# Gate and value of the last eight slices as seven block products, on input tiles of 768 tokens

## The chip, the cores and the metric

The kernel runs on one core of a Trainium2 chip. TensorE (PE) multiplies, VectorE (DVE), ScalarE (ACT) and GpSimd (POOL) work elementwise, SyncE (SP) issues the DMAs. The metric is the device time of one execution in microseconds; before the change its median over 3 runs is 1119.23 us (1118.88 to 1119.54).

## The reference

An attention with landmark means (Nystrom) over 8 batches, 8 heads, 576 tokens and 64 columns a head, whose output is the input of a gated MLP on 4608 tokens (model 512, hidden 1536):

```python
A = sm(q, k_lm); Bm = sm(q_lm, k_lm); C = sm(q_lm, k)      # 32 landmarks
for _ in range(6):
    Z = 2 * Z - Z @ Bm @ Z
attn = A @ Z @ C @ v                                       # -> x [4608, 512]
xn = x / sqrt(mean(x * x) + 1e-6) * rms_g
g = xn @ w_gate; val = xn @ w_val                          # 512 -> 1536 each
out = (g * sigmoid(g) * val) @ w_out                       # 1536 -> 512
```

The weights come as 64-bit floats and are decoded to 32 bits on the chip. Each 32-bit operand of the MLP is split into a high and a low float32r part, and a product is three matmuls: high x high, high x low, low x high.

## The kernel before

The hidden size is cut into 12 slices of 128. The kernel has two passes over the tokens, in chunks of 512 (nine in all).

**The early pass** does the attention and, chunk by chunk as the tokens become ready, the MLP of slices 0 to 3 (`early`). A partial sum [128 tokens x 512] is copied from PSUM by ACT (L294) and written to DRAM (`p_dram`, DMA pd<-ob). **The late pass** (L705 to L721) loads each chunk's inputs again (xf<-xd), splits them on ACT and DVE (L719, L720), computes slices 4 to 11, adds the partial sum on DVE (L297) and writes the output.

`mlp_chunk` (L250) makes, for each slice, 12 matmuls for gate (psg) and 12 for value (psv): four blocks of 128 of the model dimension, three matmuls each, 512 tokens wide. Then ACT takes the Silu of the gate (L268), DVE multiplies by the value (L269), and the hidden value is split (L273, L274). When all slices of the chunk are done, 12 matmuls a slice make the four output groups of 128 tokens (pso). All matmuls go through one line, L137, and PE executes them in the order in which they are written. A matmul has a weight load (PEld) ahead of it.

**What sets the order.** `Mixer` (L211) weaves the attention and the weight decoding into the MLP. It has a clock that moves by MMT = 0.216 for each matmul of `fill` (L238), and streams that say with `yield` how long they want to wait before their next piece. NW (L491) is such a wait: in `newton` (L463) it stands between the transposes, sums and maxima on DVE (BT, den) and the first product p0 (L492, the trace calls it p). WAIT1 and WAIT2 space the weight decoding of the late pass. ACT and DVE also work in one fixed order each, which a list scheduler makes at build time; PE's order is kept as written.

`Weights.load_next` (L176) decodes one 128 x 512 weight block: Abs on ACT (L187), four DVE operations (L188 to L195), then the split into high and low (L201, L202).

## Time and profile before

| | |
|---|---|
| median of 3 runs | 1119.23 us |
| profiled execution, its own time | 1122.06 us |
| its span, first to last instruction | 1120.3 us |
| first matmul of the late pass | at 528.0 us |
| PE, DVE, ACT busy over the span | 93%, 51%, 27% |
| DVE busy from 528 us on | 188.9 of 592 us |
| granted PE clock, mean; from 528 us on | 0.959; 1.00 |

A row of the timeline is: start, length, engine, line, operation, output <- inputs, sizes, count. Matmuls are pipelined, so a matmul's length (0.39 us for 512 columns) is longer than the step from one to the next; the step is read from the starts. A row of the groups ends with the busy time, the mean in ns, and the idle time of the engine ahead of it with what ended it. A window's row has the busy time and count of each engine, the granted clock and the DMA share.

### The profile page before, as it was taken

How to read it: one execution, taken by the hardware profiler on the slowest of the kernel's cores; microseconds unless marked ns; L12 is line 12 of the kernel's file. 1: busy time of each engine (PE TensorE's matmuls, PEld its weight loads, DVE VectorE, ACT ScalarE, POOL GpSimd, SP SyncE). 2: the span in 40 equal slices, each digit the busy share in tenths (PEclk: the TensorE clock that was granted, in tenths of full speed). 3: DMA queues.
4: the chain of work that ended last, by engine and by line, in shares of the span. 5: the costliest groups of instructions: out<-in, count | busy, mean ns of one | idle time of the engine just before them, and what ended most of it. 6: DMA issues, size and time to landing. Idle time of an engine off the chain costs nothing.

```text
span 1120.3 us, 16081 instructions
## 1 busy us (share of the span) xinstructions
PE 1046.4 (93%) x6630; PEld 812.7 (73%) x6630; DVE 568.9 (51%) x1203; ACT 301.8 (27%) x614; POOL 87.6 (8%) x85
## 2 busy tenths in 40 slices
PE   5559888998998999999999999999999999999998
PEld 3336555675666677777788888888888888888887
DVE  7899978566666353799832423233232323323231
ACT  3446565445344433344110101111010111100010
POOL 2243121111021010100000000000000000000000
PEclk7669988998999899999999999999999999999999
DMA  9345533314211110664311030201102020010101
GB/s 328 124 161 167 174 133 123 123 59 139 96 60 43 39 61 20 249 194 147 130 57 57 3 111 1 82 31 57 57 6 107 1 85 29 20 57 1 38 1 38
DMA packets 44457, 95.41 MB, mean 85 GB/s; under 512 B 4832, under 2 KB 24288, under 8 KB 42208
## 3 DMA queue, kind: packets, MB, share of 16 engines
q1 hardware_dynamic: 44384, 94.39, 24.6%
q8 instruction: 52, 0.85, 0.3%
q14 instruction: 21, 0.17, 0.1%
HBM read 66.06 MB, written 28.31 MB: 84 GB/s over the span
## 4 chain that ended last, share of the span: by engine, by line
PE 73%; DVE 16%; DMA 5%; ACT 3%; issue 2%; POOL 1%; SPq 0%; ACTq 0%; DVEq 0%; POOLq 0%
PE psg L137 23%; PE pso L137 22%; PE psv L137 22%; DVE lmT L345 2%; PE pO L137 1%; DVE xr L590 1%; DVE w L192 1%; DMA qk<-in_q_dram 1%; PE pn L137 1%; DMA wrawg<-in_moe_w_gate_dram 1%; DMA wrawv<-in_moe_w_val_dram 1%; DVE w L195 1%; DVE h L274 1%; PE sC L137 1%; DVE mx L379 1%
## 5 line engine op out<-in xcount | busy, mean ns | idle before, releaser
L137 PE MATMUL pso<-whio,h 128*128 128x512 f32 x864 | 279.5, 399 | 3.5 <-ACT h L273 2.1
L269 DVE TENSOR_TENSOR s<-s,psv 128x512 f32<-128x512 f32 x108 | 74.0, 685 | 282.3 <-PE psv L137 267.1
L268 ACT ACTIVATE s<-psg 128x512 f32<-128x512 f32 x108 | 64.4, 597 | 502.4 <-PE psg L137 502.2
L137 PEld LDWEIGHTS pso<-whio,h 128*128 128x128 f32 x864 | 165.5, 192 | 41.9 <-ACT h L273 3.4
L137 PE MATMUL psg<-xhi,whig 128*128 128x512 f32 x432 | 173.3, 401 | 16.4 <-ACT xhi L616 16.4
L137 PE MATMUL psg<-xlo,whig 128*128 128x512 f32 x432 | 172.6, 400 | 2.6 <-DVE xlo L618 1.9
L137 PE MATMUL pso<-wloo,h 128*128 128x512 f32 x432 | 173.1, 401 | 0.0
L137 PE MATMUL psg<-xhi,wlog 128*128 128x512 f32 x432 | 172.5, 399 | 0.0
L137 PE MATMUL psv<-xhi,whiv 128*128 128x512 f32 x432 | 170.2, 394 | 0.0
L137 PE MATMUL psv<-xlo,whiv 128*128 128x512 f32 x432 | 169.9, 393 | 0.0
L137 PE MATMUL psv<-xhi,wlov 128*128 128x512 f32 x432 | 169.6, 393 | 0.0
L137 PEld LDWEIGHTS psg<-xhi,whig 128*128 128x128 f32 x432 | 82.1, 190 | 36.2 <-ACT xhi L616 16.9
L137 PEld LDWEIGHTS psg<-xlo,whig 128*128 128x128 f32 x432 | 82.1, 190 | 22.3 <-DVE xlo L618 2.7
L297 DVE TENSOR_TENSOR ob<-pt,pso 128x512 f32<-128x512 f32 x36 | 24.6, 687 | 144.6 <-PE pso L137 144.6
L137 PEld LDWEIGHTS psg<-xhi,wlog 128*128 128x128 f32 x432 | 82.1, 190 | 19.6 <-issue 2.5
L137 PEld LDWEIGHTS pso<-wloo,h 128*128 128x128 f32 x432 | 82.8, 192 | 17.7
L137 PEld LDWEIGHTS psv<-xhi,whiv 128*128 128x128 f32 x432 | 81.2, 188 | 18.6 <-issue 1.4
L137 PEld LDWEIGHTS psv<-xlo,whiv 128*128 128x128 f32 x432 | 81.3, 188 | 18.0 <-issue 0.8
L137 PEld LDWEIGHTS psv<-xhi,wlov 128*128 128x128 f32 x432 | 81.0, 188 | 18.0 <-issue 1.3
L274 DVE TENSOR_TENSOR h<-s,h 128x512 fp32r<-128x512 f32 x108 | 76.0, 704 | 10.7 <-ACT h L273 8.6
L618 POOL TENSOR_TENSOR xlo<-xr,xhi 128x512 fp32r<-128x512 f32 (+7 forms) x32 | 31.8, 1009 | 201.3 <-ACT xhi L616 201.1
L137 PE MATMUL pn<-PV 32*32 32x96 f32 (+1 forms) x768 | 27.1, 261 | 18.6 <-DVE PV L501 14.1
(135 smaller groups left out, 995.5 us busy)
## 6 DMA issues: line engine op xcount, KB each, us to landing
xd<-xr SPq DMA_DIRECT2D x8, 1152.0 KB, 4.5
pd<-ob SPq DMA_DIRECT2D x36, 256.0 KB, 2.6
pt<-pd SPq DMA_DIRECT2D x9, 1024.0 KB, 5.2
out_dram<-ob SPq DMA_DIRECT2D x36, 256.0 KB, 2.0
vt<-in_v_dram SPq DMA_DIRECT2D x16, 512.0 KB, 4.0
qk<-in_q_dram SPq DMA_DIRECT2D x14, 576.0 KB, 4.5
qk<-in_k_dram SPq DMA_DIRECT2D x14, 576.0 KB, 5.6
wrawg<-in_moe_w_gate_dram SPq DMA_DIRECT2D x12, 512.0 KB, 3.5
```

Of the source, the lines that this page charges most:

```text
L137: tc.keep_in_program_order(nc.tensor.matmul(*args, **kw))
L192: nc.vector.scalar_tensor_tensor(w, whead, 0x3FFFFFFF, w, op0=ALU.bitwise_or, op1=ALU.bitwise_and)
L195: nc.vector.scalar_tensor_tensor(w, wtail, 29, w, op0=ALU.logical_shift_right, op1=ALU.bitwise_or)
L268: nc.scalar.activation(s, banks[0], AF.Silu)
L269: nc.vector.tensor_mul(s, s, banks[1])
L274: nc.vector.tensor_sub(h2, s, h1.bitcast(F32))
L297: nc.vector.tensor_add(ob, part[:, t, :], ps)
L345: nc.vector.tensor_reduce(lmT[:, z], qk[z].rearrange("p h (m c) -> p h m c", c=LM), axis=AX.X, op=ALU.add)
L379: nc.vector.tensor_reduce(mx[:, e : e + 1], sC[e], axis=AX.X, op=ALU.max)
L590: last = nc.vector.scalar_tensor_tensor(xr[:, kk], xr[:, kk], gsb[:, kk : kk + 1], Rt, op0=ALU.mult, op1=ALU.mult)
L618: eng.tensor_sub(xlo[:, kk, off : off + n], xr[:, kk, pos : pos + n], xhi[:, kk, off : off + n].bitcast(F32),)
```

## The change

Slices 4 to 11 get another algorithm for gate and value. Write the weights of a slice as a 2 x 2 matrix of blocks (gate and value by the two halves of the model dimension, A11 A12 / A21 A22) and the inputs of 768 tokens as another (halves of the model dimension by two tiles of 384 tokens, B11 B12 / B21 B22). The four result blocks, gate and value of the two token tiles, then take seven block products instead of eight, in Winograd's form: P1 = A11 B11, P2 = A12 B21, and five products of combined blocks. A block product is 2 x 3 = 6 matmuls of 384 columns.

- `Fast.stream` decodes gate and value of a slice, combines them on DVE into S1 to S4 and splits seven blocks of 256 columns (high on ACT, low on DVE).
- `prepare` combines the inputs of a unit of 768 tokens in place and splits seven blocks of 768 columns (x1 to x7).
- `unit` writes the products of a slice into the banks px, pz and pw in the order 1, 5, 6, 2, 3, 7, with 4 of the slice before it after 5. Products 6, 7 and 4 are added to the bank of product 1, product 3 to that of 5. Between them ACT copies what a bank holds so far (c1, c2, c3) and DVE adds the next sum to the copy. The hidden values are then split, 384 columns at a time.
- The late pass becomes two passes of four slices each, over six units. The first adds to the early partial sums and writes a second set (`p2_dram`), the second adds to that and writes the output. Partial sums are loaded three groups ahead, 256 KB each.
- The first unit's inputs are prepared in the last early chunk, between its gate and value and its output products (`between`). The weights of the second pass's first slice and its output weights go to tiles of the early ones; three slices are decoded into tiles that come free in the sixth unit (`refill`).
- The pools: early inputs get a pool that is closed before `prepare`, attention pools move to the other end of SBUF, and a tile of 32 bytes is put in front of the late pool, so that its tiles start at multiples of 64 bytes. The attention tiles at that end start at 32 bytes past such a multiple.
- NW becomes 6.0, WAIT2 2.5.

The diff, cut to its core:

```diff
-NW = 2.0
+NW = 6.0
...
 WAIT1 = 4.0
-WAIT2 = 3.2
+WAIT2 = 2.5
...
+    mxs = ExitStack()
+    mx_ = mxs.enter_context(tc.tile_pool(name="mx", bufs=2, reuse_waits="tile"))
...
-    p_dram = [dram.tile([P, T // P, DM], F32, name=f"pd{i}", tag=f"pd{i}") for i in range(NCH)]
+    NG = NT // P
+    p_dram = [dram.tile([P, DM], F32, name=f"pd{i}", tag=f"pd{i}") for i in range(NG)]
+    p2_dram = [dram.tile([P, DM], F32, name=f"pe{i}", tag=f"pe{i}") for i in range(NG)]
...
+        between()
...
-                    if part is None:
-                        nc.scalar.copy(ob, ps)
-                        nc.sync.dma_start(p_dram[i][:, t, :], ob)
-                    else:
-                        nc.vector.tensor_add(ob, part[:, t, :], ps)
-                        r0 = T * i + t * P
...
+                    nc.scalar.copy(ob, ps)
+                    nc.sync.dma_start(p_dram[i * (T // P) + t], ob)
...
+    with tc.tile_pool(name="ap", bufs=1, side="right") as ap, tc.tile_pool(
+        name="sm", bufs=2, side="right"
     ) as sm, tc.tile_pool(name="pa", bufs=8 - GB, space=PSUM) as pa:
...
-            mix.fill(mlp_chunk(i, early, fs, *chunks.pop(i), None))
+            mix.fill(mlp_chunk(i, early, fs, *chunks.pop(i)))
             mix.drain(lambda: stage["second"] > i)
...
-    lp = ctx.enter_context(tc.tile_pool(name="lp", bufs=1))
-    late["p"] = lp
-    fl = list(range(NFA, NF))
-    later = Weights([(f, f if f < 2 * NFA else f - 2 * NFA) for f in fl])
-    later.plan([(f, nm) for f in fl[:NFA] for nm in "gvo"])
-    mix.add(later.stream(WAIT1))
-    for i in range(B - 1, NCH):
-        mix.fill(mlp_chunk(i, early, fs, *chunks.pop(i), None))
-    mix.drain(lambda: False)
-    later.plan([(f, nm) for f in fl[NFA:] for nm in "gv"] + [(f, "o") for f in fl[NFA:]])
-    mix.add(later.stream(WAIT2))
-    for i in range(NCH):
-        xf = lp.tile([P, NK, T], F32, name="xf", tag="xf", bufs=1)
+
+    al = ctx.enter_context(tc.tile_pool(name="al", bufs=1, side="right"))
+    nc.gpsimd.memset(al.tile([P, 8], F32, name="pad", tag="pad"), 0.0)
+    lp = ctx.enter_context(tc.tile_pool(name="lp", bufs=1, side="right", reuse_waits="tile"))
+    pl = ctx.enter_context(tc.tile_pool(name="pl", bufs=1, space=PSUM, reuse_waits="tile"))
+
+    TS = 384
+    NU = NT // (2 * TS)
+    SMMT = MMT * TS / T
...
+        def split(self, tile_, src):
+            nc.scalar.copy(tile_[:, 0], src)
+            nc.vector.tensor_sub(tile_[:, 1], src, tile_[:, 0].bitcast(F32))
...
+                self.fetch(f, "g")
+                self.fetch(f, "v")
+                yield -wait
+                g = self.decode(f, "g")
+                yield -wait
+                v = self.decode(f, "v")
+                yield -wait
+                ts = [place(c) for c in range(7)]
+                g0, g1, v0, v1 = g[:, : NK // 2], g[:, NK // 2 :], v[:, : NK // 2], v[:, NK // 2 :]
+                self.split(ts[A11], g0)
+                self.split(ts[A12], g1)
+                self.split(ts[A22], v1)
+                nc.vector.tensor_add(v1, v0, v1)
+                nc.vector.tensor_sub(v0, g0, v0)
+                yield -wait
+                nc.vector.tensor_sub(g0, v1, g0)
+                nc.vector.tensor_sub(g1, g1, g0)
+                self.split(ts[S1], v1)
+                self.split(ts[S3], v0)
+                self.split(ts[S2], g0)
+                self.split(ts[S4], g1)
+                self.done[f, "gv"] = ts
+                yield -wait
...
+        def get(self, f, what):
+            while (f, what) not in self.done:
...
+    gv_tags = [f"w{hl}{nm}{s}" for s in range(NFA) for hl in ("hi", "lo") for nm in "gv"]
+    o_tags = [(f"whio{s}", f"wloo{s}") for s in range(NFA)]
+    spare = gv_tags[7:]
+    lslot = [slot(lp, [f"fs{s}c{c}" for c in range(7)]) for s in range(NFA)]
+    fa, fb = list(range(NFA, 2 * NFA)), list(range(2 * NFA, 3 * NFA))
+    plan_a = [(f, "gv", lslot[s]) for s, f in enumerate(fa)]
+    plan_a += [(f, "o", oslot(lp, (f"lo{s}0", f"lo{s}1"))) for s, f in enumerate(fa)]
+    plan_b = [(fb[0], "gv", slot(wp, gv_tags[:7]))]
+    plan_b += [(f, "o", oslot(wp, o_tags[s])) for s, f in enumerate(fb)]
...
-        part = lp.tile([P, T // P, DM], F32, name="pt", tag="pt", bufs=2)
-        nc.sync.dma_start(part, p_dram[i])
-        xhi = mp.tile([P, NK, T], F32R, name="xhi", tag="xhi", bufs=XB)
-        xlo = mp.tile([P, NK, T], F32R, name="xlo", tag="xlo", bufs=XB)
-        for kk in range(NK):
-            nc.scalar.copy(xhi[:, kk], xf[:, kk])
-            nc.vector.tensor_sub(xlo[:, kk], xf[:, kk], xhi[:, kk].bitcast(F32))
-        mix.fill(mlp_chunk(i, later, fl, xhi, xlo, part))
+        return xf
...
+    def prepare(xf, xs):
+
+        h = NK // 2
+        b11, b12 = xf[:, :h, :TS], xf[:, :h, TS:]
+        b21, b22 = xf[:, h:, :TS], xf[:, h:, TS:]
+
+        def split(p, src):
+            t = lxs[0].tile([P, 2, h, TS], F32R, name=f"x{p}", tag=f"x{p}", bufs=1)
+            nc.scalar.copy(t[:, 0], src)
+            nc.vector.tensor_sub(t[:, 1], src, t[:, 0].bitcast(F32))
+            xs[p] = t
+
+        split(1, b11)
+        nc.vector.tensor_sub(b11, b12, b11)
+        split(5, b11)
+        yield
+        nc.vector.tensor_sub(b11, b22, b11)
+        split(6, b11)
+        yield
+        split(2, b21)
+        yield
+        split(3, b22)
+        nc.vector.tensor_sub(b12, b22, b12)
+        yield
+        split(7, b12)
+        yield
+        nc.vector.tensor_sub(b21, b21, b11)
+        split(4, b21)
...
+    of = {1: A11, 2: A12, 3: S4, 4: A22, 5: S1, 6: S2, 7: S3}
+
+    def product(ps, ws, xs, p, start):
+
+        w, x = ws[of[p]], xs[p]
+        h = NK // 2
+        for kk in range(h):
...
+                mm(
+                    ps,
+                    w[:, a, kk],
+                    x[:, b, kk],
+                    start=start and kk == a == b == 0,
+                    stop=kk == h - 1 and a == 1,
+                    skip_group_check=not start,
...
+    def unit(u, fs, xs, hs, src, last, after):
...
+        def close(fi, c1, px, ws):
+            yield from product(px, ws, xs, 4, False)
+            nc.vector.tensor_mul(c1, c1, px)
+            hs[fi, 0] = hidden(fi, 0, c1)
...
+        for fi, f in enumerate(fs):
+            ws = fast.get(f, "gv")
+            px = pl.tile([P, TS], F32, name="px", tag="px", bufs=2)
+            pz = pl.tile([P, TS], F32, name="pz", tag="pz", bufs=2)
...
+            yield from product(px, ws, xs, 1, True)
+            nc.scalar.copy(c1, px)
+            yield from product(pz, ws, xs, 5, True)
+            nc.scalar.copy(c3, pz)
+            if pend:
+                yield from close(*pend.pop())
+                after(fi - 1)
+            yield from product(px, ws, xs, 6, False)
+            nc.scalar.copy(c2, px)
+            pw = pl.tile([P, TS], F32, name="pw", tag="pw", bufs=1)
+            yield from product(pw, ws, xs, 2, True)
+            nc.vector.tensor_add(c1, c1, pw)
+            nc.scalar.activation(c1, c1, AF.Silu)
+            yield from product(pz, ws, xs, 3, False)
+            nc.vector.tensor_add(c2, c2, pz)
+            nc.scalar.activation(c2, c2, AF.Silu)
+            yield from product(px, ws, xs, 7, False)
+            nc.vector.tensor_add(c3, c3, px)
+            nc.vector.tensor_mul(c2, c2, c3)
+            hs[fi, 1] = hidden(fi, 1, c2)
+            pend.append((fi, c1, px, ws))
...
+        groups = list(range(half, ng)) + list(range(half))
+        nxt = prepare(load_next.pop(), xs_next) if load_next else iter(())
...
+        def part(t):
+            g = u * ng + t
+            ob = mp.tile([P, DM], F32, name="ob", tag=("ob", "s")[g % 2])
+            nc.sync.dma_start(ob, src[g])
...
+        def store(t):
+            g, ob = u * ng + t, obs[t]
+            nc.vector.tensor_add(ob, ob, bank.pop(t))
+            if not last:
+                nc.sync.dma_start(p2_dram[g], ob)
+                return
+            nc.sync.dma_start(out[g * P : (g + 1) * P, :], ob)
...
+        for t in groups[:3]:
+            part(t)
+        for fi in range(nf - 1):
+            yield from out_mm(groups[0], fi)
+        yield from close(*pend.pop())
+        after(nf - 1)
+        next(nxt, None)
+        for fi in range(nf - 1):
+            yield from out_mm(groups[1], fi)
+        next(nxt, None)
+        for n in (0, 1):
+            yield from out_mm(groups[n], nf - 1)
+            store(groups[n])
+            part(groups[n + 3])
+            next(nxt, None)
+        for n in range(2, ng):
+            for fi in range(nf):
+                yield from out_mm(groups[n], fi)
+            store(groups[n])
+            if n + 3 < ng:
+                part(groups[n + 3])
+            next(nxt, None)
+        for _ in nxt:
+            pass
+
...
+    xs_next, load_next, lxs = {}, [], []
+    mix.add(fast.stream(plan_a[:NFA], WAIT1))
+    for i in range(B - 1, NCH):
+        if i == NCH - 1:
+            first_x = load_x(0)
...
+        def between(i=i):
+            if i < NCH - 1:
+                return
+            mxs.close()
+            lxs.append(ctx.enter_context(tc.tile_pool(name="lx", bufs=1, reuse_waits="tile")))
+            for _ in prepare(first_x, xs_next):
+                pass
+            mix.add(fast.stream(plan_a[NFA:], WAIT1))
+
+        mix.fill(mlp_chunk(i, early, fs, *chunks.pop(i), between))
+    mix.add(fast.stream(plan_b, 2 * WAIT1))
+    freed = set()
+
+    def refill():
+        for s, f in enumerate(fb[1:]):
+            while s not in freed:
+                yield -0.3
+            yield from fast.stream([(f, "gv", lslot[s])], WAIT2)
+
+    mix.add(refill())
+    for n in range(2 * NU):
+        u, second_pass = n % NU, n >= NU
+        xs, hs = dict(xs_next), {}
+        xs_next = {}
+        if n + 1 < 2 * NU:
+            load_next.append(load_x((n + 1) % NU))
+        after = (lambda fi: freed.add(fi)) if n == NU - 1 else (lambda fi: None)
+        mix.fill(
+            unit(u, fb if second_pass else fa, xs, hs, p2_dram if second_pass else p_dram,
+                 second_pass, after),
+            SMMT,
+        )
```

How the order moves. On PE in the early pass, around p0 (the trace's p) of the seventh batch; sC and sA are scores of a later stage, pso is an output product of the fourth chunk. Before:

```order
L137 MATMUL pso<-wloo_1157,h_3354 128x512
L137 MATMUL pso<-whio_1156,h_3354 128x512
L137 MATMUL p_3545<-BT 32x32 x8
L137 MATMUL pso<-whio_1223,h_3429 128x512
L137 MATMUL pso<-wloo_1224,h_3429 128x512
L137 MATMUL pso<-whio_1223,h_3429 128x512
...
L137 MATMUL pso<-whio_1223,h_3429 128x512
L137 MATMUL sC<-qk_3417,lmT 32x288
L137 MATMUL sA<-qk_3417,lmT 32x288
...
L137 MATMUL sC<-lmT 32x32 x4
L137 MATMUL pso<-whio_1269,h_3525 128x512
L140 MATMUL sE<-ident,E 128x128 x4
```

Now:

```order
L141 MATMUL pso<-whio_1317,h_3591 128x512
L141 MATMUL sC<-qk_3482,lmT 32x288
L141 MATMUL sA<-qk_3482,lmT 32x288
...
L141 MATMUL sC<-lmT 32x32 x4
L141 MATMUL pso<-wloo_1318,h_3591 128x512
L144 MATMUL sE<-ident,E 128x128 x4
L144 MATMUL sF<-ident,E 64x128
L141 MATMUL pso<-whio_1317,h_3591 128x512
L141 MATMUL p_3696<-BT 32x32 x8
L141 MATMUL pso<-whio_1317,h_3591 128x512
```

p0 stood 15 MLP matmuls earlier, and ahead of the scores; now the scores and the first transposes (sE, sF) go first.

On PE in the late pass, one slice's gate and value; x1 to x7 are the split inputs, swfs0c0 the first combined weight block of the slot. Before, the gate's first three matmuls and the value's:

```order
L137 MATMUL psg_6794<-xhi_6752,whig5_5046 128x512
L137 MATMUL psg_6794<-xlo_6753,whig5_5046 128x512
L137 MATMUL psg_6794<-xhi_6752,wlog5_5047 128x512
...
L137 MATMUL psv_6807<-xhi_6752,whiv5_5085 128x512
L137 MATMUL psv_6807<-xlo_6753,whiv5_5085 128x512
L137 MATMUL psv_6807<-xhi_6752,wlov5_5086 128x512
```

Now, with the next slice's first two products:

```order
L141 MATMUL px_6479<-x1_6363,swfs0c0_5092 128x384 x6
L141 MATMUL pz_6480<-x5_6367,swfs0c4_5096 128x384 x6
L141 MATMUL px_6479<-x6_6381,swfs0c5_5097 128x384 x6
L141 MATMUL pw_6505<-x2_6391,swfs0c1_5093 128x384 x6
L141 MATMUL pz_6480<-x3_6401,swfs0c2_5094 128x384 x6
L141 MATMUL px_6479<-x7_6422,swfs0c6_5098 128x384 x6
L141 MATMUL px_6544<-x1_6363,swfs1c0_5263 128x384 x6
L141 MATMUL pz_6545<-x5_6367,swfs1c4_5267 128x384 x6
L141 MATMUL px_6479<-x4_6443,swfs0c3_5095 128x384 x6
L141 MATMUL px_6544<-x6_6381,swfs1c5_5268 128x384 x6
```

24 matmuls of 512 columns for 512 tokens have become 42 of 384 for 768 tokens, and a slice's fourth product stands after two of the next slice's.

On DVE in the sixth unit; sw are weights that are decoded for the second pass, c the copies of the accumulators, h hidden values:

```order
L727 TENSOR_SCALAR sw_7947<-sw_7947 128x512
L883 TENSOR_TENSOR c_7728<-c_7728,px 128x384
L730 SCALAR_TENSOR_TENSOR sw_7947<-srawg_7919,sw_7947 128x512
L726 TENSOR_SCALAR sw_7984<-sw_7984 128x512
L873 TENSOR_TENSOR h_7833<-c_7728,h_7833 128x384
L733 SCALAR_TENSOR_TENSOR sw_7947<-srawg_7919,sw_7947 128x512
L904 TENSOR_TENSOR c_7803<-c_7803,pw 128x384
L727 TENSOR_SCALAR sw_7984<-sw_7984 128x512
L907 TENSOR_TENSOR c_7804<-c_7804,pz 128x384
L730 SCALAR_TENSOR_TENSOR sw_7984<-srawv_7921,sw_7984 128x512
L910 TENSOR_TENSOR c_7805<-c_7805,px 128x384
L733 SCALAR_TENSOR_TENSOR sw_7984<-srawv_7921,sw_7984 128x512
```

The decoding's operations have come in between the additions to the accumulators' copies.

More of the change, by code (lines that the diff above doesn't have):

```diff
@@ L140, in tp @@
         tc.keep_in_program_order(nc.tensor.transpose(*args))
-    late = {}
     class Weights:
@@ L248, in nystrom_moe_kernel, with mlp_chunk @@
     mix = Mixer()
-    def mlp_chunk(i, wts, fs, xhi, xlo, part):
+    def mlp_chunk(i, wts, fs, xhi, xlo, between=lambda: None):
         nf = len(fs)
@@ L269, in mlp_chunk @@
                 nc.vector.tensor_mul(s, s, banks[1])
-                pool = mp if fi < NFA else late["p"]
-                h12 = pool.tile([P, 2, T], F32R, name=f"h{fi}", tag=f"h{fi}", bufs=1)
+                h12 = mp.tile([P, 2, T], F32R, name=f"h{fi}", tag=f"h{fi}", bufs=1)
                 h1, h2 = h12[:, 0], h12[:, 1]
-                (nc.scalar.copy if part is None else nc.vector.tensor_copy)(h1, s)
+                nc.scalar.copy(h1, s)
                 nc.vector.tensor_sub(h2, s, h1.bitcast(F32))
@@ new lines, in hidden, with out_mm @@
+    def hidden(fi, t, s):
+        if t == 0:
+            h12 = mp.tile([P, 2, T], F32R, name=f"h{fi}", tag=f"h{fi}", bufs=1)
+            hi, lo = h12[:, 0, :TS], h12[:, 1, :TS]
+        else:
+            hi, lo = (
+                wp.tile([P, T], F32R, name=f"h{fi}{n}", tag=spare[2 * fi + n], bufs=1)[:, :TS] for n in range(2)
+            )
+        nc.scalar.copy(hi, s)
+        nc.vector.tensor_sub(lo, s, hi.bitcast(F32))
+        return hi, lo
+    def unit(u, fs, xs, hs, src, last, after):
+        nf = len(fs)
+        pend = []
+        def close(fi, c1, px, ws):
[6 more added lines that the diff above has]
+            pz = pl.tile([P, TS], F32, name="pz", tag="pz", bufs=2)
+            c1, c2, c3 = (
+                lp.tile([P, TS], F32, name=f"c{n}", tag=f"c{n}", bufs=2 if n == 1 else 1) for n in (1, 2, 3)
+            )
+            yield from product(px, ws, xs, 1, True)
[19 more added lines that the diff above has]
+            pend.append((fi, c1, px, ws))
+        ng = 2 * TS // P
+        half = ng // 2
+        groups = list(range(half, ng)) + list(range(half))
+        nxt = prepare(load_next.pop(), xs_next) if load_next else iter(())
+        bank, obs = {}, {}
+        def part(t):
+            g = u * ng + t
+            ob = mp.tile([P, DM], F32, name="ob", tag=("ob", "s")[g % 2])
+            nc.sync.dma_start(ob, src[g])
+            obs[t] = ob
+        def out_mm(t, fi):
+            if t not in bank:
+                bank[t] = pg.tile([P, DM], F32, name="pso", tag="pg")
+            hi, lo = fast.get(fs[fi], "o")
+            h12 = hs[fi, t // half]
+            sl = slice(t % half * P, (t % half + 1) * P)
+            mm(bank[t], h12[0][:, sl], hi, start=(fi == 0), stop=False)
+            yield
+            mm(bank[t], h12[0][:, sl], lo, start=False, stop=False)
+            yield
+            mm(bank[t], h12[1][:, sl], hi, start=False, stop=(fi == nf - 1))
+            yield
+        def store(t):
[29 more added lines that the diff above has]
+            pass
```

89 lines of the change are left out of this document (72 added, 17 removed).

## The prediction

> **What bounds the kernel now.** First the page: span, engines, and the chain that ended last.
>
> ```profile
> span 1120.3 us, 16081 instructions
> PE 1046.4 (93%) x6630; PEld 812.7 (73%) x6630; DVE 568.9 (51%) x1203; ACT 301.8 (27%) x614; POOL 87.6 (8%) x85
> PE 73%; DVE 16%; DMA 5%; ACT 3%; issue 2%; POOL 1%; SPq 0%; ACTq 0%; DVEq 0%; POOLq 0%
> ```
>
> PE is busy for 93% of the span and holds 73% of the chain. A mean over both passes hides where PE is the limit, so next come the windows by stage (columns: PE, PEld, DVE, ACT, POOL busy with counts, granted clock, DMA share, GB/s).
>
> ```profile
> 139.00:215.00 76.00, 65.76 (x691) 43.10 (x692) 60.80 (x149) 39.43 (x84) 17.67 (x16) 0.87 0.38 130
> 215.00:269.00 54.00, 48.18 (x420) 35.30 (x418) 32.71 (x80) 24.14 (x55) 7.08 (x7) 0.94 0.30 98
> 269.00:326.00 57.00, 52.26 (x523) 36.97 (x522) 37.80 (x95) 25.54 (x58) 9.76 (x9) 0.97 0.26 92
> 528.00:1120.00 592.00, 588.52 (x2593) 486.07 (x2591) 188.90 (x318) 61.99 (x107) 0.00 (x0) 1.00 0.14 47
> ```
>
> The last row is the late pass. PE does not pause, the clock is full, DVE is at 32% and DMA at 14%. So there the number and the pace of matmuls set the time. The early rows are mixed: PE pauses and DVE works at 60 to 80%. The pace is read from the timeline of PE in the late pass, first and last of 15 rows:
>
> ```profile
> 799.73 0.39 PE L137 MATMUL psv<-xlo,whiv 128*128 128x512 f32 x1
> ...
> 802.90 0.39 PE L137 MATMUL psg<-xhi,whig 128*128 128x512 f32 x1
> ```
>
> Fourteen steps in 3.17 us are 0.2264 us; with 2592 matmuls (9 chunks of 8 slices of 36) in the 588 us that PE is busy, 0.2267. The 0.39 is a pipelined duration and no pace.
>
> **The change, part by part.** *Gate and value.* A slice on 768 tokens costs 36 matmuls of 512 columns before (24 x 1.5) and 7 x 6 = 42 of 384 after. There are 48 such slice-units (6 units, 8 slices). No row has 384 columns, so the pace lies between the 512 step and that of pO with 288 columns, here on PE and on the weight loads:
>
> ```profile
> 378.04 0.53 PE L137 MATMUL pO<-AS,Whi 64*128 64x288 f32 x4
> 378.41 0.29 PE L137 MATMUL pO<-AS,Wlo 64*128 64x288 f32 x2
> 378.28 0.19 PEld L137 LDWEIGHTS pO<-AS,Wlo 64*128 64x128 f32 x2
> ```
>
> The second pair of the first row ends at 378.57 and, at 0.29 each, began at 378.28; the next pair began at 378.41: 0.13 us for 288 columns (two half-height matmuls run side by side, so a pair is one step). From 288 to 512 columns, 0.13 to 0.2267, the line is 0.43 ns a column; at 384 it gives 0.172 to 0.173. I take 0.173. The bounds: 0.170 if the whole step shrinks with the columns (0.2267 x 0.75), 0.19 if the weight load, whose own rows last 0.19, became the pace. The third row speaks against that: the load began at 378.28 and its matmul at 378.41.
>
> Before: 48 x 36 x 0.2267 = 391.7 us. After: 48 x 42 x 0.173 = 348.8. The output products stay, 48 x 18 matmuls. **Gain 43**; bounds 49 (0.170) and 9 (0.19).
>
> The Trainium skill, "TensorE: Matmul & The Clock Gate", section "Back-to-back issue gap", gives N / 2.4 + 2.5 ns when warm: 215.8 ns at 512 columns, where this trace has 227, so the measurement decides. By the page, an estimate, 48 x (36 x 0.2158 - 42 x 0.1625) = 45 us would be gained.
>
> *What the products add on the other engines.* Each slice-unit now has on DVE three additions, two multiplications and two subtractions of 384 columns, on ACT three copies, two Silu and two casts. Each unit has seven splits of combined inputs (a cast on ACT, a subtraction on DVE) and four combinations on DVE, all of 768 columns, and six output additions. The nearest rows:
>
> ```profile
> L720 DVE TENSOR_TENSOR xlo<-xf,xhi 128x512 fp32r<-128x512 f32 x36 | 24.1, 685 | 0.0
> L422 DVE TENSOR_TENSOR AS<-AT,AS 128x576 fp32r<-128x576 f32 x16 | 12.0, 751 | 3.0 <-ACT AS L421 2.9
> L524 DVE TENSOR_TENSOR Wlo<-pW,Whi 128x256 fp32r<-128x256 f32 x8 | 3.3, 417 | 6.5 <-ACT Whi L523 6.5
> L268 ACT ACTIVATE s<-psg 128x512 f32<-128x512 f32 x108 | 64.4, 597 | 502.4 <-PE psg L137 502.2
> L556 ACT COPY xr<-pO 128x288 f32<-128x288 f32 x64 | 22.3, 405 | 21.4 <-PE pO L137 21.1
> ```
>
> From 256 to 512 and 576 columns DVE takes about 1.04 ns a column: 0.55 us for 384, 0.95 for 768. ACT at 384 lies between 0.405 and 0.597, about 0.49. A unit lasts 4 x (42 x 0.173 + 18 x 0.2267) = 45.4 us on PE; DVE needs 28 x 0.55 + 11 x 0.95 + 6 x 0.69 = 30.0 us, ACT under 20. This fits on average, so I cost it at nothing in the ten units without weight work. What hides it is PE's next products: a sum read from a bank has two to four products (1.04 us each) before that bank is written again. The tightest place is the first slice of a unit, where ACT's copy of product 1 has only product 5 to hide behind: 1.04 us against 0.49 and a semaphore on each side. If that cover went, 12 x 0.5 = 6 us.
>
> *Weights.* A slice now needs, beside two decodings, four combinations and seven splits of 256 columns:
>
> ```profile
> L188 DVE TENSOR_SCALAR w<-w 128x512 f32<-128x512 f32 x36 | 17.6, 488 | 8.8 <-ACT w L187 8.6
> L189 DVE TENSOR_SCALAR w<-w 128x512 int32<-128x512 int32 x36 | 16.9, 470 | 0.3
> L192 DVE SCALAR_TENSOR_TENSOR w<-wrawv,w 128x512 int32<-128x512 int32 x12 | 9.1, 758 | 0.2
> L195 DVE SCALAR_TENSOR_TENSOR w<-wrawg,w 128x512 int32<-128x512 int32 x12 | 8.2, 686 | 0.1
> ```
>
> That is 2 x 2.40 + 11 x 0.42 = 9.4 us of DVE a slice. Three slices are refilled in the sixth and seventh units, and in DVE's order their operations stand between the accumulator additions that PE waits for. Counted from the second slice of the sixth unit to the first of the seventh, DVE has 53 us of work in 45.4 us of PE. PE's lead of two products (2 us) takes some of the 7.6; the rest is late there. Around the first unit, where inputs and weights are prepared together, the backlog by the same count is at most 4 us. Bounds 0 and 11.6 us, with the handover above 17.6; I take **8 lost**, nearer the DVE count than nothing, since the order is fixed and DVE can't step aside.
>
> *DMA.* 28 MB more (inputs read twice, a second set of partial sums written and read) over some 550 us is 50 GB/s, beside 47 in the late row at a share of 0.14. It goes to 0.3 and stays covered. All of it is on SP's queue, where a store waits for its addition and holds up the loads behind it:
>
> ```profile
> pd<-ob SPq DMA_DIRECT2D x36, 256.0 KB, 2.6
> ```
>
> The partial sums are asked for three groups of 12 output matmuls (8 us) ahead, against 2.6 to land and 2.7 behind a store. I cost it at nothing; without that cover, 2.6 us a group.
>
> *The early pass.* NW moves p0 back. PE waits there, from 200 to 400 us:
>
> ```profile
> PE p L137 <- DVE BT L466: 13.2, 3, 5.8
> PE pn L137 <- DVE PV L501: 2.0, 1, 2.0
> ```
>
> p0 now stands 13, 15 and 21 matmuls later (the first pair of fences on the order shows the 15), which is 2.9 to 4.8 us at 0.2267, and behind a block of scores besides; the longest of the three waits is 5.8. The first pn keeps its place, so the Newton chain has less room, not a later end. Bounds 0 (DVE, at 60 to 65%, is only late somewhere else) and 13.2; I take **10 gained**. Attention tiles now start at 32 bytes past a multiple of 64; no row shows such a start. It could cost nothing; at most I allow a second fixed part per step, which by the line above is about 0.01 us (0.2267 - 0.43 x 0.512), for the 6630 - 3888 = 2742 attention matmuls, which run some seven side by side: 4 us. I take **1 lost**.
>
> **Sum.** On the profiled execution: 1120.3 - 43 + 8 - 10 + 1 = 1076.3 us of span. That execution reports 1122.06, 1.8 above its span and 2.8 above the median of 1119.23; on the median the same 44 us give **1075**.
>
> **Rivals.** *More than that*: steps of 0.170, nothing lost on DVE, all 13.2 gained: 1119 - 49 - 13 = 1057. For: the late pass shows no pause of PE now. Against: 0.13 at 288 columns is more than 0.75 x 0.2267 x 288 / 384 = 0.1275.
>
> *DVE becomes the bound*: all 11.6 us at the weights, 1.2 us in each of twelve units because inputs, accumulators and hidden values queue in one fixed order, no early gain: 1119 - 43 + 26 = 1102. For: in the last slice of each unit the order gives DVE 7.7 us of work against 7.2 of PE. Against: the slices before it have 4 to 5.
>
> *Weight loads set the pace* (0.19): 1119 - 9 + 8 - 9 = 1109. Against: the 0.13 above. The same page of the Trainium skill, section "The mechanism" of part 3, says that a load overlaps a running matmul only if its row group differs; by it 0.19 would add to each step, and a step of 0.2267 for 512 columns rules that out.
>
> *The accumulators' handovers, slower*: products 6, 7 and 4 are added to a bank that ACT or DVE has just read, three times a slice-unit. It decides from (43 + 9) / 48 = 1.1 us a slice-unit on. At 0.45 a handover, 1.35 in all, the loss is 65: 1119 - 52 + 65 = 1132. For: ACT and DVE each work in one order, and a 0.83 us input cast can stand before a 0.49 copy. Against: two products of cover at most of them. A pace that doesn't shrink below 0.194 would end there too; that the change does less than it says is excluded by the order, which has 42 products' matmuls a slice-unit.
>
> *Early pass loses*: p0 delayed makes the attention stages end later, and four chunks wait 2 us each: 1119 - 43 + 8 + 8 = 1092.
>
> **How the numbers follow.** The forecast 52 in 100, its own range 1064 to 1088. More 12, DVE bound 21, weight loads 5, early loss 3, handovers 7, of which 1 ends within 0.2%. 1054 to 1107 leaves out a third of "more" (4), a quarter of "DVE bound" (5), half of "weight loads" and nearly all of the handovers: 2 in 10. Below 0.2% (2 us) this measurement can't tell a change. Faster 0.93, same 0.01, slower 0.06.
>
> **What will show it.** In the late pass the starts of px, pz and pw 0.173 apart (0.170, 0.19 or 0.2267 name the rival) and a unit of 45.4 us. Idle time of PE before px and pso, put down to DVE, of some 8 us and mostly in the first, sixth and seventh units; if it is spread evenly, it is the fixed order, and if it is put down to ACT's copies, the handovers. The waits of p for BT near zero and the late pass starting about 9 us earlier, near 519. Steps in the late pass that vary without waits, or a clock below 1.00, would make all of this wrong.

## The result, and the profile after

The changed kernel takes 1069.49 us (median of 4 runs, 1064.2 to 1074.22), the kernel before 1119.38 in the same job: a ratio of 0.955, with a 95% interval of 0.9504 to 0.9596. The profiled execution after took 1069.73 us. First its page: span, busy time of the engines, and the chain that ended last.

```profile
span 1067.6 us, 17593 instructions
PE 1005.0 (94%) x6918; PEld 838.9 (79%) x6918; DVE 738.9 (69%) x1503; ACT 485.2 (45%) x988; POOL 90.0 (8%) x86
PE 74%; DVE 17%; DMA 3%; ACT 3%; issue 2%; POOL 1%; SPq 0%; ACTq 0%; DVEq 0%; POOLq 0%
```

PE issues 288 matmuls more than before and is busy 41 us less. DVE has 170 us of work more, ACT 183, and yet their shares of the chain hardly changed, 17% beside 16 and 3% beside 3: most of the work that the products added there is hidden. The units below show how much.

Where the 52.7 us between the two spans come from is read by stage. The windows of the kernel after (columns as in the prediction): two stages of the early pass, then the first, second, third with fourth, sixth and seventh units of the late pass, and the rest.

```profile
209.00:258.00 49.00, 47.76 (x453) 34.09 (x452) 31.40 (x85) 24.74 (x55) 8.44 (x8) 1.00 0.33 108
258.00:313.00 55.00, 52.33 (x509) 37.14 (x507) 37.80 (x98) 25.36 (x57) 9.44 (x9) 0.97 0.27 95
515.00:561.00 46.00, 46.00 (x243) 43.03 (x242) 40.95 (x72) 25.07 (x47) 0.00 (x0) 1.00 0.48 157
561.00:608.00 47.00, 45.68 (x240) 42.49 (x240) 30.15 (x49) 19.24 (x36) 0.00 (x0) 1.00 0.40 134
608.00:699.00 91.00, 91.00 (x481) 85.24 (x480) 57.09 (x90) 37.57 (x70) 0.00 (x0) 1.00 0.31 102
745.00:790.00 45.00, 45.00 (x239) 42.19 (x238) 39.35 (x79) 25.89 (x53) 0.00 (x0) 1.00 0.35 119
790.00:836.00 46.00, 46.00 (x244) 43.03 (x243) 34.65 (x62) 20.60 (x42) 0.00 (x0) 1.00 0.32 103
836.00:1064.00 228.00, 227.91 (x1201) 213.11 (x1199) 133.91 (x215) 88.87 (x168) 0.00 (x0) 1.00 0.29 97
```

The late pass starts at 515.3 us, 12.7 earlier than before, and with the last stores takes 552.3 us in place of 592.3: 40.0 less. In it PE pauses once, in the second unit (45.68 of 47). Ten units take 45.57 us from their first matmul to the next unit's, the second takes 47.19, and the last 45.35 to the start of its last matmul. In the first and sixth units DVE is busy for 41 and 39 us and PE misses nothing.

The pause, in the timeline of PE, ACT and DVE around 573 us (a bracket gives the idle time ahead and what ended it):

```profile
571.26 1.20 PE L141 MATMUL pw<-x,swfs1c 128*128 128x384 f32 x6
572.26 0.66 ACT L725 ACTIVATE sw<-srawv 128x512 f32<-128x512 f32 x1 [2.41 <-DMA srawv<-in_moe_w_val_dram]
572.30 1.21 PE L141 MATMUL pz<-x,swfs1c 128*128 128x384 f32 x6
572.95 0.43 DVE L726 TENSOR_SCALAR sw<-sw 128x512 f32<-128x512 f32 x1 [3.08 <-ACT sw L725]
573.30 0.55 DVE L883 TENSOR_TENSOR c<-c,px 128x384 f32<-128x384 f32 x1
573.88 0.51 ACT L872 CAST h<-c 128x384 fp32r<-128x384 f32 x1 [0.96 <-DVE c L883]
574.29 0.47 ACT L901 COPY c<-px 128x384 f32<-128x384 f32 x1
574.82 0.44 PE L141 MATMUL px<-x,swfs1c 128*128 128x384 f32 x1 [1.32 <-ACT c L901]
```

Two things are in these rows. The products pw and pz start 1.04 us apart with six matmuls between: a step of 0.173 us at 384 columns. And PE's px is late because ACT and DVE are. Each does its work in one fixed order. In ACT's, the Abs (L725) of a weight that `refill` decodes for the second pass stands here, in the second unit of the first; it waits 2.41 us for that weight's DMA. In DVE's, the decoding's next step (L726) stands here too and waits 3.08 us for the Abs, with the multiplication by the bank's sum (L883) behind it. ACT's split (L872) waits for that product, and the copy (L901), for which PE waits, stands behind the split.

The waits of PE after, over the whole program (total, times, longest):

```profile
PE pn L141 <- DVE PV L497: 6.6, 6, 1.6
PE pso L141 <- DVE h L274: 3.2, 4, 1.1
PE pso L141 <- ACT h L273: 2.8, 3, 1.6
PE px L141 <- ACT c L901: 1.3, 1, 1.3
PE p L141 <- DVE BT L462: 0.6, 1, 0.6
```

The three waits of p for BT, 13.2 us in all, are gone (the 0.6 lies before the first early chunk). Longer than before is the wait at the end of the last early chunk, where pso waits some 2.5 us for the last hidden values (h on ACT 1.6, on DVE 0.9; before, 0.8 and 0.4): ACT does two of the casts of `prepare` and DVE two of its subtractions first.

### The profile page after: what moved, and what is told of

The parts are those of the page before. It is cut to its first block, busy times and chain, and to the rows that moved or that the text cites. A ratio compares the mean times of both kernels' runs of the same rounds, so it can differ in the third digit from the quotient of the medians.

```text
span 1067.6 us, 17593 instructions
## 1 busy us (share of the span) xinstructions
PE 1005.0 (94%) x6918; PEld 838.9 (79%) x6918; DVE 738.9 (69%) x1503; ACT 485.2 (45%) x988; POOL 90.0 (8%) x86
## 4 chain that ended last, share of the span: by engine, by line
PE 74%; DVE 17%; DMA 3%; ACT 3%; issue 2%; POOL 1%; SPq 0%; ACTq 0%; DVEq 0%; POOLq 0%
PE pso L141 24%; PE px L141 18%; PE pz L141 9%; PE psg L141 6%; PE psv L141 5%; PE pw L141 4%; PE pO L141 2%; PE pn L141 2%; DVE xr L586 2%; DMA srawv<-in_moe_w_val_dram 1%; DVE lmT L341 1%; DVE h L274 1%; PE pCV L141 1%; DVE xlo L614 1%; DVE s L270 1%
## 5 line engine op out<-in xcount | busy, mean ns | idle before, releaser
L141 PE MATMUL pso<-whio,h 128*128 128x512 f32 x288 | 101.3, 421 | 6.1 <-DVE h L274 3.2
L141 PE MATMUL pso<-solo,h 128*128 128x512 f32 x432 | 100.4, 390 | 0.0
L141 PE MATMUL psg<-xhi,whig 128*128 128x512 f32 x144 | 61.1, 424 | 16.5 <-ACT xhi L612 16.5
L141 PEld LDWEIGHTS pso<-whio,h 128*128 128x128 f32 x288 | 57.0, 200 | 22.7 <-DVE h L274 5.1
L872 ACT CAST h<-c 128x384 fp32r<-128x384 f32 x96 | 49.5, 515 | 34.5 <-DVE c L883 28.2
L141 PE MATMUL psg<-xlo,whig 128*128 128x512 f32 x144 | 60.9, 423 | 2.8 <-DVE xlo L614 2.5
L141 PE MATMUL pso<-wloo,h 128*128 128x512 f32 x144 | 60.5, 420 | 0.0
L141 PE MATMUL psg<-xhi,wlog 128*128 128x512 f32 x144 | 60.3, 419 | 0.0
L141 PE MATMUL psv<-xhi,whiv 128*128 128x512 f32 x144 | 58.4, 406 | 0.0
L141 PE MATMUL psv<-xlo,whiv 128*128 128x512 f32 x144 | 58.3, 405 | 0.0
L141 PE MATMUL psv<-xhi,wlov 128*128 128x512 f32 x144 | 57.9, 402 | 0.0
```

The lines of the kernel that those rows point to most:

```text
L141: tc.keep_in_program_order(nc.tensor.matmul(*args, **kw))
L872: nc.scalar.copy(hi, s)
```

## The experiments

### NW alone, both ways

`after_nw2` is the changed kernel with the wait of before:

```diff
-NW = 6.0
+NW = 2.0
```

> The changed kernel with NW back at 2.0, nothing else. Theory (NW made the early gain): p waits for BT again, 10 to 14 us in all, and the late pass begins 10 to 13 us later than the changed kernel's 515.3, at 525 to 528; the time is some 1080. Rival (the pools and the finer reuse waits of the early pass made it): the late pass begins at 514 to 518 all the same, and the time stays at 1070. The late pass is the same in both, 548 to 549 us.

It took 1082.56 us (1080.39 to 1086.51), a ratio of 0.9681 (0.9653 to 0.9708). Its late pass starts at 527.5, and the wait is back, as in this row of PE's waits:

```profile
PE p L141 <- DVE BT L462: 13.8, 4, 5.8
```

So the algorithm with all that hangs on it is worth 36 us, and NW 13 in the changed kernel. `before_nw6` is the kernel before with that number alone:

```diff
-NW = 2.0
+NW = 6.0
```

> The kernel before with NW = 6.0, nothing else. Theory (NW alone): the waits of p for BT fall from 13 us to about 1, the late pass begins at 514 to 518 in place of 528, and the time is 1107 to 1110. Rival (it needs the new pools): the late pass begins at 524 or later, 1116 to 1120.

It took 1099.99 us (1098.96 to 1106.65), 0.9851 (0.9813 to 0.9888): 18.8 us less, more than the three waits together, and more than the expectation had. Windows of the same stretches of the program, first of before, then of this kernel (second to third early chunk, then third to sixth):

```profile
139.00:215.30 76.30, 66.06 (x694) 43.40 (x695) 60.80 (x149) 39.64 (x85) 17.67 (x16) 0.87 0.38 130
215.30:377.70 162.40, 148.71 (x1346) 107.44 (x1344) 96.71 (x241) 71.08 (x158) 23.30 (x22) 0.95 0.23 78
```

```profile
140.10:208.10 68.00, 60.88 (x673) 41.01 (x673) 54.76 (x146) 37.30 (x83) 17.70 (x16) 0.92 0.45 150
208.10:356.80 148.70, 144.32 (x1372) 103.22 (x1365) 94.92 (x244) 71.28 (x158) 24.29 (x23) 1.00 0.24 86
```

Together 22.0 us shorter. PE's idle time, the length less its busy time, falls from 23.9 to 11.5 us: 12.4. But the busy time of the same matmuls falls as well, from 214.8 to 205.2: 9.6, as the granted clock rises from 0.87 and 0.95 to 0.92 and 1.00. (The idle time is not that of p alone: between 100 and 400 us pn's waits for PV, 8.3 us, and one of p for nsum, 1.7, go too, and new ones come, 2.7 for nden and 2.5 of pCV for PV the longest.) Why the clock rises is seen in windows of before just behind two of the waits, those that end at 255.9 and 364 us:

```profile
256.00:262.00 6.00, 6.00 (x44) 4.29 (x48) 5.06 (x14) 1.79 (x3) 1.16 (x1) 0.56 0.16 54
364.00:371.00 7.00, 6.81 (x33) 5.37 (x34) 5.02 (x17) 1.65 (x4) 2.16 (x2) 0.53 0.00 0
```

The three waits last 5.8, 4.3 and 3.1 us. With each the clock falls to half for 6.8, 3.4 and 6.8 us, of which 5.4, 3.0 and 6.3 lie behind the wait. So each cost itself and half of what lies behind, 1.5 to 3.2 us, as matmuls ran at half speed there. The Trainium skill, "TensorE: Matmul & The Clock Gate", section "What's actually happening", has the clock at 4/8 after an idle window of about 3.4 us; the stretches here, one or two times 3.4 us at half, agree, but the wait of 3.1 us is shorter than such a window.

### Where tiles start

`no_pad` leaves out the tile of 32 bytes, so that the late tiles start 32 bytes past a multiple of 64; `att_align` puts it ahead of the attention pools, so that all of them start at such a multiple.

```diff
 # no_pad: out; att_align: ahead of `with tc.tile_pool(name="ap", ...)`
-    al = ctx.enter_context(tc.tile_pool(name="al", bufs=1, side="right"))
-    nc.gpsimd.memset(al.tile([P, 8], F32, name="pad", tag="pad"), 0.0)
```

> The changed kernel without the 32-byte tile in front of the late pool, so that the block weights and half of the output weights begin at 32 bytes past a multiple of 64. If the start matters to TensorE, the steps of 384 columns go above 0.173 us or those of the output products above 0.227, in the late pass alone; at 0.01 us a step on 2016 or more matmuls the time grows by 20 us or more. If it does not, the steps and the unit of 45.57 us stay, and the time is within 5 us of 1069.

> The changed kernel with the 32-byte tile ahead of the attention's pools, so that attention tiles too begin at multiples of 64. The prediction allowed 1 us of loss for their odd start, 0 to 4. If that is so, the late pass begins 1 to 4 us earlier than 515.3; if the start does not matter, at 515 within the 3.4 us steps in which the clock is granted.

`no_pad` took 1069.78 us (0.9568, 0.9544 to 0.9593), `att_align` 1068.79 (0.9552, 0.952 to 0.9584): neither can be told from the change by its time. The units can: in `no_pad` five of the first late pass take 45.91 us, not 45.57 (the second, with its stall, 49.5), those of the second pass as in the change. The groups of the output products with that pass's output weights (solo), first after, then `no_pad`:

```profile
L141 PE MATMUL pso<-solo,h 128*128 128x512 f32 x432 | 100.4, 390 | 0.0
```

```profile
L141 PE MATMUL pso<-solo,h 128*128 128x512 f32 x432 | 102.6, 395 | 0.0
```

Only these 72 matmuls a unit, whose moving operand now starts 32 bytes off, became longer, by 0.34 us a unit, 4.7 ns each. The block products, whose weight tiles start there too but are the stationary operand, keep 0.173. So by the units the pad is worth 2 us. For the attention tiles no cost was shown: 0.7 us of median between kernels whose own runs lie 8 to 10 apart. The late pass of `att_align` starts at 510.4 us, 4.9 before the change's, which the expectation would have taken for a cost of the odd start; but that of `no_pad`, whose attention tiles start as in the change, starts at 510.7, so this sign can't tell the two.

### Weights: DVE or the order?

The prediction let DVE's 28 us of decoding in the sixth and seventh units cost 8 us. After, part of it stood in the second unit instead (the stall above). `late_fetch` ties each refill's loads to the input loads, so that decoding can't start early:

```diff
-                self.fetch(f, "g")
-                self.fetch(f, "v")
+                with tc.issue_after(loads[-1].ins) if f in fb[1:] else nullcontext():
+                    self.fetch(f, "g")
+                    self.fetch(f, "v")
...
-            nc.sync.dma_start(xf[:, :, pos : pos + n], x_dram[b][:, :, off : off + n])
+            loads.append(nc.sync.dma_start(xf[:, :, pos : pos + n], x_dram[b][:, :, off : off + n]))
```

> The changed kernel, with the loads of the three slices that are decoded again for the second pass held back until the inputs of the seventh unit have been asked for; nothing else. In the changed kernel the scheduler had put the first of these decodings into the second unit, where ACT waited 2.4 us for its DMA with an accumulator's copy behind it, and PE waited 1.3. Theory (that is the whole stall of the second unit): the second unit falls from 47.2 us to 45.6. The same run puts all three decodings, 28 us of DVE, into the sixth and seventh units. If the prediction's price for that was right, those two units now grow by 5 us or more in all; if DVE's backlog is taken up by the output phases, they stay at 45.6 within 1 us.

It took 1070.28 us in a single run. Windows of the second unit, of 46 us across the sixth and seventh, where the prediction counted, and of the seventh:

```profile
563.00:609.00 46.00, 46.00 (x244) 43.03 (x243) 28.57 (x45) 18.79 (x35) 0.00 (x0) 1.00 0.33 110
752.00:798.00 46.00, 46.00 (x245) 43.11 (x244) 45.38 (x93) 26.89 (x57) 0.00 (x0) 1.00 0.45 144
791.00:837.00 46.00, 46.00 (x244) 43.06 (x243) 36.20 (x67) 21.36 (x43) 0.00 (x0) 1.00 0.36 115
```

The stall of the second unit is gone, so its cause was the weight's place in the orders of ACT and DVE. And with all the decoding where the prediction had it, DVE is full, 45.4 of 46 us, and PE loses nothing: units of 45.57 and 45.60. In the trace of these two units DVE starts to read px, pz, pw and pso at most 1.4 us after the product's last matmul, in a unit without weights at most 1.3: the sums that PE waits for aren't late.

### How much cover is left: DVE, ACT and the tile size

Two kernels repeat one operation of `prepare` with the same result, to load one engine: `dve_x3` each subtraction three times (13.3 us of DVE a unit more), `act_x3` each cast three times (11.6 us of ACT).

```diff
 # dve_x3 (act_x3: the loop over the copy instead)
             nc.scalar.copy(t[:, 0], src)
-            nc.vector.tensor_sub(t[:, 1], src, t[:, 0].bitcast(F32))
+            for _ in range(3):
+                nc.vector.tensor_sub(t[:, 1], src, t[:, 0].bitcast(F32))
```

> The changed kernel, with each of the seven subtractions that split a unit's inputs done three times over (same result): 14 x 0.95 = 13.3 us more DVE a unit, 42 of 45.6 in place of 28.6. If DVE's work is hidden as a sum (its output phase has room, and the scheduler moves the new work there), the ten units without weights stay within 0.5 us of 45.57, and the time grows by under 10 us. If DVE's one order is what decides, as the rival had it, each unit grows by 2 us or more, and the time by 24 or more.

It took 1125.82 us in a single run, 56 more. PE's waits in its late pass, and that pass as one window:

```profile
PE pso L141 <- DVE ob L942: 32.3, 13, 3.9
PE px L141 <- DVE x L827: 4.8, 1, 4.8
```

```profile
520.00:1124.00 604.00, 562.75 (x2867) 519.50 (x2867) 500.12 (x776) 239.50 (x449) 0.00 (x0) 0.97 0.30 98
```

DVE is busy for 83%, not for all of the time, and yet eight of the twelve units take 48.5 to 50.1 us, and three 51 to 59. As a sum the work would fit; in the fixed order the repeated subtractions stand among the output additions (ob), those free the banks of pso, and PE waits there. Three rows of DVE and one of PE in the fourth unit:

```profile
710.55 0.68 DVE L942 TENSOR_TENSOR ob<-ob,pso 128x512 f32<-128x512 f32 x1
711.15 5.30 DVE L827 TENSOR_TENSOR x<-xf,x 128x768 fp32r<-128x768 f32 x6
718.10 0.68 DVE L942 TENSOR_TENSOR ob<-ob,pso 128x512 f32<-128x512 f32 x1
718.84 4.49 PE L141 MATMUL pso<-solo,h 128*128 128x512 f32 x12 [2.66 <-DVE ob L942]
```

The pauses cost clock as well: 0.97.

> The changed kernel, with each of the seven casts that split a unit's inputs done three times over: 14 x 0.83 = 11.6 us more ACT a unit, some 30 of 45.6 in place of 18.7. The rival on handovers said that a long cast standing before an accumulator's copy makes PE wait, as at 573 us in the changed kernel. If so, the longer casts in the last slice of a unit and the first of the next cost 1 us or more a unit, 12 in all. If the two to four products of cover suffice, the units stay at 45.57 within 0.3 us.

It took 1068.14 us in a single run. Its wait of PE from 500 us on, and windows of the start of the late pass and of all from the second unit on:

```profile
PE px L141 <- ACT c L895: 5.1, 1, 5.1
```

```profile
507.00:520.00 13.00, 7.29 (x29) 6.32 (x28) 9.10 (x14) 11.84 (x21) 0.00 (x0) 0.74 0.40 118
561.00:1063.00 502.00, 501.66 (x2642) 469.49 (x2640) 325.52 (x538) 309.36 (x543) 0.00 (x0) 1.00 0.33 105
```

From 561 us on PE misses 0.3 of 502 us with ACT at 62%: the copies between products have room for 11.6 us more a unit. Only the first unit pays (53.77 us): there the repeated casts of the preparation stand in ACT's order ahead of the copy of product 1.

`ts256` makes the token tiles 256 wide (nine units of 512 tokens a pass), to have a third size of matmul:

```diff
-    TS = 384
+    TS = 256
...
-            part(groups[n + 3])
+            if n + 3 < ng:
+                part(groups[n + 3])
```

> The changed kernel with token tiles of 256 (units of 512 tokens, nine a pass). The step at 256 columns tells the fixed part of a step from its part by columns: a fixed 0.013 us and 0.417 ns a column give 0.120; in proportion to 0.227 at 512 it would be 0.113, to 0.173 at 384 it would be 0.115; if the weight load, 0.19 by its rows, set the pace, 0.19. With 0.120 a unit is 4 x (42 x 0.120 + 12 x 0.2267) = 31.0 us and the late pass 18 x 31.0 = 559, some 11 us more than with 384.

It took 1081.11 us in a single run. Two groups of its timeline of PE:

```profile
640.52 0.88 PE L141 MATMUL px<-x,swfs1c 128*128 128x256 f32 x6
641.24 0.88 PE L141 MATMUL pz<-x,swfs1c 128*128 128x256 f32 x6
```

Six steps in 0.72 us: 0.120. With 0.173 at 384 and 0.2267 at 512 the three lie on one line, 0.417 ns a column and 13 ns a matmul. The weight load, 0.19 us a row, sets no pace even at 0.120. Fifteen of the eighteen units take 31.1 us, where 31.0 was expected; the first of each pass takes 34.4 and the second unit 32.1, with waits of PE for ACT's copies and for weights.

### A version that beats both, and what of it is explained

`after_again` is the changed kernel once more; `h_first_late` has the order of `late_fetch` and lets the preparation of the first unit stand behind the last early chunk's split of the hidden values:

```diff
-                nc.scalar.copy(h1, s)
-                nc.vector.tensor_sub(h2, s, h1.bitcast(F32))
+                split_ins[:] = [nc.scalar.copy(h1, s), nc.vector.tensor_sub(h2, s, h1.bitcast(F32))]
...
-            for _ in prepare(first_x, xs_next):
-                pass
+            with tc.issue_after(split_ins[0].ins), tc.issue_after(split_ins[1].ins):
+                for _ in prepare(first_x, xs_next):
+                    pass
```

> The changed kernel itself once more, beside the next run. Its four times so far spread over 10 us (1064 to 1074), the kernel before over 2.4. Theory: the spread is the granted clock in the early pass, which drops to a half for 3.4 us or a multiple after some of PE's pauses; each such stretch costs 1.7 us, so time and mean clock move together, and the late pass is the same in every profile.

> The changed kernel with the second pass's loads held back, as in the run before, and with ACT and DVE made to split the last early chunk's hidden value before they start on the first unit's inputs. In the changed kernel that value stood behind two casts (1.6 us) and two subtractions (1.8 us) of 768 columns; PE waited 2.5 us at 502 to 505 us, and the clock was halved for 6.8 us after it, 3.4 us more. Theory: the wait is gone and the late pass begins 2 us (with the clock, 5 us) earlier; the first unit may give back up to 1 us, since its inputs are ready 1.8 us later. With the 1.6 us of the second unit, 1062 to 1067 beside 1069. Rival (the wait only moves to the first unit): unit 0 grows by as much as the wait was.

`after_again` took 1068.33 us (1063.96 to 1070.62), 0.9533 (0.951 to 0.9556). Its late pass takes 552.5 us, as in the change's profile; its times and mean clocks go together only roughly (1063.96 and 1068.33 us both at 0.966). `h_first_late` took 1061.05 (1059.91 to 1066.65), 0.9473 (0.9452 to 0.9495). The intervals don't touch. But the waits that its profile lacks are only the 1.3 us of px (1.6 in PE's starts) and 0.7 of DVE's h at the end of the last chunk; ACT's h still takes 1.6 there. Two more kernels took each order alone:

> The changed kernel with only one of the two orders of the version that beat it: the preparation of the first unit stands behind the last early chunk's split of the hidden values, and the weight loads stay where the change has them. The version with both took 1061.05 us against 1068.33. Theory (the two orders gain only the waits that they remove, and the rest of the 7 us is the granted clock of the early pass, which differs from one execution to the next): 0.7 us are removed here, so 1067 to 1068, with the stall of 1.6 us at the second unit still there. Rival (a pause of PE at the end of the early pass also halves the clock for 3.4 us or more after it, so a wait of 1 us is worth 2 to 4 us): 1063 to 1065, and no stretch of half clock between 500 and 515 us in the profile.

> The changed kernel with only the other order: the refilled weights are loaded behind the input loads of the unit. Theory: 1.6 us of stall at the second unit go, so 1066 to 1067. Rival: the stall is followed by a stretch of half clock in most executions (one profile showed 3.4 us of it at 572 us, two others none), so 1064 to 1065. If neither order alone gets below 1065, the 7 us of the version with both aren't the sum of these waits, and stay with the clock's scatter in the early pass.

`h_first_alone` took 1063.95 us (0.9505, 0.9488 to 0.9522), `late_fetch_timed` 1065.56 (0.9514, 0.9495 to 0.9532). By its median the first lies 4 us under `after_again`, as the rival expected, but the two ran in different jobs and the intervals of their ratios overlap. By its profile it isn't the rival's win either, as the last chunk's end runs at full clock in it and in `after_again` alike. Its late pass has longer stalls than the change (first two units 47.0 and 49.2 us), and what it gained lies ahead of anything that was edited. The ninth early chunk starts at 471.4 us in the one and at 478.1 in the other. In windows up to that chunk, `h_first_alone` first, then `after_again`:

```profile
0.00:471.40 471.40, 414.82 (x3895) 293.37 (x3896) 341.18 (x834) 228.59 (x498) 89.93 (x86) 0.93 0.37 126
```

```profile
0.00:478.10 478.10, 421.48 (x3894) 297.36 (x3895) 342.57 (x834) 228.96 (x498) 88.98 (x86) 0.91 0.37 124
```

Up to there the work and its order are the same on PE, DVE and ACT. PE's idle time is 56.6 us in both; its matmuls take 414.8 us in the one and 421.5 in the other, at a granted clock of 0.93 and 0.91. So the clock makes the 6.7 us. Of the 7 us between `h_first_late` and `after_again`, then, 2.3 are shown to come from waits removed. The medians of the two orders alone, 4.4 and 2.8 us under `after_again`, add up to the 7, which is also what two real gains would give. But one profile of each was taken, and mean clocks differ from run to run (0.960 to 0.971 over the five runs of `h_first_late`, 0.960 to 0.966 of `after_again`). Whether the edit had a part in the clock stays open.

## Why the prediction was right, and where it wasn't

**Total.** Forecast 1075, measured 1069.49. Two terms were off, and both in the same direction; of *more than that*, the rival on that side, two parts came true (no loss at DVE's backlog, all of the early waits) and one, the step of 0.170, didn't. So the hit doesn't come of errors that cancelled. But the 5.5 us that are left lie within the 10 over which the executions of this one kernel spread, so the total alone would not have shown which terms were off.

**Gate and value, 43 gained: right.** The step is 0.173, as taken from the line between 288 and 512 columns. A unit takes 45.57 us where the same steps made 45.4, which is 2 us over twelve units.

**DVE's and ACT's additional work at nothing: right.** DVE is busy for 28.5 us in a unit without weights (57.09 in two; 30.0 worked out), ACT for 18.8. The handover from which a loss was bounded at 6 us, ACT's copy behind one product in the first slice, isn't seen in any of the ten even units, and `act_x3` shows that it isn't close.

**"8 lost" at the weights: wrong, and it is the step that failed.** The prediction reasoned that 53 us of DVE's work in 45.4 of PE's must come out late. In `late_fetch` that work stands there and DVE is full, 45.4 of 46 us, as counted; but PE loses nothing that can be read (0.4 us in the second execution of that order, whose sixth unit took 46.01). The prediction let the backlog fall on the sums that PE waits for, and those come as promptly there as elsewhere (1.4 us after the product at most). What comes late must then be what PE needs later, such as the weights of the next slices; that is inferred, not read in a row. The one loss after, 1.6 us in the second unit, had a cause that the prediction didn't name: a decoding that the scheduler put early in the orders of ACT and DVE and that waits for its DMA with the accumulators' work behind it. The late pass, forecast 43 - 8 = 35 shorter, became 40.0 shorter.

**NW, 10 gained: the mechanism right, the size short.** In the changed kernel it is worth 13, the upper bound; alone 18.8, beyond it. The wait itself was the sum's only term: of the 22.0 us that `before_nw6` gains between the second and the sixth early chunk, 12.4 are idle time and 9.6 slower matmuls behind the pauses. The windows that the prediction quoted had the clock at 0.94 and 0.97 in just those stages. Why more of it came through in the kernel before than in the changed one isn't settled. The clock bears on it: from 210 us on it is 1.00 in the profile of `before_nw6`, and 0.98 from 210 to 515 us in the profile after, behind the end of the last chunk among other places; but that is one profile of each.

**Attention tiles, 1 lost: not shown.** `att_align` doesn't differ from the change. The pad, which sets the start of the late tiles, keeps off a loss of 2 us; the prediction gave no price to such a start in the late pass.

**DMA at nothing: right.** The share is 0.29 to 0.48, and no wait of PE in the late pass leads to a DMA but the one for the refilled weight.

**The rivals.** *Weight loads set the pace* falls with 0.173, and finally with 0.120. The prediction gave the rule of the Trainium skill, "TensorE: Matmul & The Clock Gate", section "The mechanism", too narrowly: the section names a background weight buffer beside the row group, and with that the overlap that the trace shows is no contradiction. *Handovers* fall with the even units and `act_x3`. *DVE becomes the bound* is false at this load, but its mechanism is real: `dve_x3` shows that a fixed order binds before the sum does, some 4 us a unit from 13 us of additional work, though mostly at the output additions (32.3 of the 39.4 us of PE's waits) and not where inputs and accumulators meet. *Early pass loses* falls: p0's delay took the waits away, and what came in their place (PE for nden 2.7 us, for PV 2.5) is smaller.

## What to carry to other kernels

A long pause of PE costs more than its length: look at the granted clock in the windows behind it, and price both. A full engine is no loss by itself; look in its fixed order for the operation that waits for a DMA, or that frees a bank, with work behind it that PE needs soon. And when an edit moves the time, look whether the profile moved at the edited place: here 6.7 us between two profiles were the clock's alone.

## What the runs showed of the hardware

- With pauses of 3.1 to 5.8 us PE's granted clock fell to half for 3.4 or 6.8 us. Shorter ones did so too at times: the 2.5 us at the end of the last early chunk was followed by 6.8 us of half clock in the profile after, which brings that window to 0.91, and by none in `after_again` (1.00), as these two rows show, after first:

```profile
476.00:515.00 39.00, 36.54 (x147) 29.32 (x146) 31.87 (x60) 20.68 (x40) 0.00 (x0) 0.91 0.35 112
```

```profile
476.00:515.00 39.00, 36.48 (x162) 29.76 (x161) 31.46 (x59) 20.90 (x41) 0.00 (x0) 1.00 0.37 125
```

  The same program thus takes several microseconds more or less from one execution to the next.
- A matmul of 512 columns whose moving operand starts 32 bytes past a multiple of 64 took 4.7 ns longer; for the stationary operand no difference was seen.
- In a stream of the MLP's matmuls, each with its own weight load, a step is 0.417 ns a column and 13 ns: 0.120, 0.173 and 0.2267 us at 256, 384 and 512 columns.
